# Two batches that take turns on the feed-forward weights: from runs of 8, 16, 8 blocks to runs of 4, 8, 8, 8, 4

## The chip, the cores and the metric

The kernel runs on one core of one Trainium2 chip. The metric is the device time of one execution in microseconds (us), as a median of several runs; less is better. PE is the matrix engine, PEld its weight loads, DVE the vector engine, ACT the scalar engine, SP the engine that issues the DMAs. PSUM is the memory that PE writes to, SBUF the on-chip working memory.

## What is computed

The reference is two stages of attention followed by a feed-forward layer, all in float32 (the inputs are float64 in memory for the two weight matrices, and are turned into float32 on the chip):

```
def sm_attn(qq, kk, vv):
    s = scale * matmul(qq, kk^T);  a = softmax(s);  return a @ vv
p_packed = sm_attn(p, k, v)                 # 32 packed rows per head
out      = sm_attn(q, p_packed, p_packed)
x = out as (B*S, H*D)
h = x @ w_in;  g = h * tanh(softplus(h));  result = g @ w_out
```

There are 8 batches of 8 heads, 576 tokens and a head size of 64; 32 packed rows per head; the feed-forward layer goes from 512 to 2048 (d_ff) and back to 512. h * tanh(softplus(h)) is the Mish function, one ACT instruction here.

## The kernel before

The kernel works batch by batch. For a batch, the attention yields the second-stage softmax weights, transposed, in a high and a low half (`aT_hi`, `aT_lo`: a value and what rounding to the matmul type leaves of it). The second value product is never made alone: `packed_w` (line 428) multiplies the packed values (`ppT`) with a chunk of 512 columns of w_in, again split into halves (`wp_hi` on ACT, `wp_lo` on DVE, lines 446 and 447), and the up-projection multiplies those with `aT`.

**Blocks and steps.** d_ff is cut into 16 blocks of 128. `order` (line 571) lists (batch, block) pairs; a *step* t works on pair t. In a step (line 605) PE makes the up-projection of pair t (`up`, line 477: two halves of 288 tokens, 6 matmuls each, from a PSUM tile `ps_h` through Mish into `g`), and, two steps late (LAG = 2), the down-projection of pair t - 2 (`down`, line 525: four accumulators of 128 tokens, three matmuls each, from the halves `g_hi`, `g_lo` made at lines 498 and 499). Of the 576 tokens, 512 go this way; the last 64 of two batches are gathered over four blocks and multiplied together by `down_rest` (line 545), as soon as both batches have gone through those four blocks.

**Turns.** Batches 2 to 7 go through all 16 blocks in a row. Batches 0 and 1 share the opening, while the weights are still being converted. Line 27 gives their runs:

```
TURNS = [(0, 0, 8), (1, 0, 16), (0, 8, 16)]      # (batch, first block, end)
```

At the end of a run that doesn't end a batch, `evac` (line 509) copies the four accumulators into SBUF tiles `part`; at the end of the batch they are added (line 516) and written out.

**Weight conversion.** w_in and w_out arrive as float64 words. 32 conversions (lines 352 to 419) turn them into float32: 16 of w_in (four chunks of 512 columns by four row blocks) and 16 of w_out (one for each block of d_ff). One conversion is a DMA into a staging tile `w_st` (`fetch`), two ACT instructions (`words`, lines 385 and 386), four DVE instructions (`join`, lines 390 to 397) and `done`: for w_out a cast to the high half on ACT (line 418) and the low half on DVE (line 419), for w_in a DMA that puts every second result into DRAM (line 402), from where batches 2 to 7 and the later turns read it. The list `weights` (line 580) gives the sequence: w_in chunk 0, w_out 0 and 1, w_in chunk 1, w_out 2 to 7, w_in chunk 2, w_out 8, w_in chunk 3, w_out 9 to 15. `conversion` (line 585) hands out half conversions, and `take(conv, n)` places n of them at a point of the program: two in most steps, 42 in all ahead of step 16.

**Order on the engines.** PE's order is the program's order throughout. Until step 16 (START) that holds for DVE, ACT and SP too: every queue is executed in the order written, and an instruction that waits holds up all behind it. From step 16 on the framework orders DVE and ACT by readiness and priority. The attention of batch 1 (`second`) is written out by hand between steps 0 to 4; that of batch 2 is a generator that is stepped from step 20 on (line 613), up to three pieces a step, and must be through by step 30.

## Time and profile before

| | us |
|---|---|
| median of 3 runs (lowest, highest) | 804.06 (804.03, 805.2) |
| the profiled execution | 805.43 |
| its span, first to last instruction | 803.6 |
| PE busy | 765.4 (95%) |
| DVE busy | 441.7 (55%) |
| ACT busy | 322.7 (40%) |

A profile is of one execution. Busy time is the sum of an engine's instruction times; on PE, neighbouring matmuls overlap, so its instructions start closer together than they are long. A row of a timeline gives start, duration, engine, line, operation and tiles; in brackets, how long the engine had been idle and what ended that wait. A row of waits gives who waited for whom, the total, the count and the longest. A row of grouped instructions gives the count, the busy total and the mean in ns. The granted clock is the share of PE's full clock.

### The profile page before, as it was taken

Reading aid. Unit: us, or ns where it says so; the run is one execution under the profiler, and the core shown is the slowest. Engines: PE = TensorE matmul, PEld = TensorE weight load, DVE = VectorE, ACT = ScalarE, POOL = GpSimd, SP = SyncE. Lnnn points to the kernel's source line nnn. Section 1 sums busy time; section 2 is a strip of 40 time slices with the busy share of each in tenths; the row PEclk is TensorE's granted clock in tenths of the full one; section 3 lists DMA queues with packets and bytes.
Section 4 is the critical chain, followed back from the end, with each engine's and each line's share of the span. In section 5 each row is a group of like instructions: output and inputs, shape, how many; then the busy total and the mean of one; then the engine's idle time right before and its main releaser. Section 6 shows DMA issues by size and latency. Waiting matters only on the chain.

```text
span 803.6 us, 13720 instructions
## 1 busy us (share of the span) xinstructions
PE 765.4 (95%) x5584; PEld 610.2 (76%) x5584; DVE 441.7 (55%) x846; ACT 322.7 (40%) x752; POOL 0.7 (0%) x6
## 2 busy tenths in 40 slices
PE   7767689999999999999999999999999999999997
PEld 5445478877887787878788787878788787878886
DVE  5787777696467447353553546444463545542332
ACT  4364557563433424244333433334252343222221
POOL 0000000000000000000000000000000000000000
PEclk7578799999999999999999999999999999999999
DMA  9994105434423441152311541243311501131002
GB/s 263 282 331 156 37 27 171 163 113 118 142 82 117 149 140 56 53 171 79 93 53 61 175 114 60 69 154 112 113 53 53 148 30 54 53 105 53 1 1 66
DMA packets 42814, 85.82 MB, mean 107 GB/s; under 512 B 8448, under 2 KB 26880, under 8 KB 42752
## 3 DMA queue, kind: packets, MB, share of 16 engines
q1 hardware_dynamic: 42752, 84.95, 34.5%
q8 instruction: 44, 0.72, 0.4%
q14 instruction: 18, 0.15, 0.1%
HBM read 71.30 MB, written 13.63 MB: 106 GB/s over the span
## 4 chain that ended last, share of the span: by engine, by line
PE 86%; DVE 8%; ACT 2%; DMA 2%; issue 1%; SPq 0%; DVEq 0%; ACTq 0%
PE ps_h L486 24%; PE acc L503 15%; PE acc L505 14%; PE acc L504 14%; PE ps_kq L120 4%; PE ps_w L435 4%; PE ps_s L129 3%; PE ps_rest L503 2%; PE ps_rest L505 2%; PE ps_rest L504 2%; DMA w_st<-in_moe_w_out_dram 2%; PE ps_pp L260 2%; PE ps_a L251 1%; DVE wo L394 1%; DVE wo L397 1%
## 5 line engine op out<-in xcount | busy, mean ns | idle before, releaser
L503 PE MATMUL acc<-wo,g_hi 128*128 128x512 f32 x512 | 214.6, 419 | 8.0 <-ACT wo L418 5.9
L489 ACT ACTIVATE g<-ps_h 128x288 f32<-128x288 f32 (+1 forms) x256 | 98.2, 384 | 279.7 <-PE ps_h L486 229.1
L504 PE MATMUL acc<-wo,g_hi 128*128 128x512 f32 x512 | 202.9, 396 | 0.2 <-DVE wo L419 0.2
L505 PE MATMUL acc<-wo,g_lo 128*128 128x512 f32 x512 | 203.0, 396 | 0.1
L486 PE MATMUL ps_h<-aT_hi,wp_hi 128*128 128x288 f32 x512 | 158.1, 309 | 2.8 <-ACT g L489 1.8
L498 DVE CAST g_hi<-g 128x512 fp32r<-128x512 f32 x112 | 47.7, 426 | 195.0 <-ACT g L489 195.0
L486 PE MATMUL ps_h<-aT_hi,wp_lo 128*128 128x288 f32 x512 | 152.7, 298 | 1.8 <-DVE wp_lo L447 1.8
L486 PE MATMUL ps_h<-aT_lo,wp_hi 128*128 128x288 f32 x512 | 152.6, 298 | 0.0
L503 PEld LDWEIGHTS acc<-wo,g_hi 128*128 128x128 f32 x512 | 96.9, 189 | 50.3 <-issue 24.0
L505 PEld LDWEIGHTS acc<-wo,g_lo 128*128 128x128 f32 x512 | 97.1, 190 | 22.9 <-DVE g_lo L499 0.5
L486 PEld LDWEIGHTS ps_h<-aT_hi,wp_hi 128*128 128x128 f32 x512 | 97.8, 191 | 19.0 <-issue 5.7
L486 PEld LDWEIGHTS ps_h<-aT_lo,wp_hi 128*128 128x128 f32 x512 | 98.0, 191 | 8.8
L504 PEld LDWEIGHTS acc<-wo,g_hi 128*128 128x128 f32 x512 | 97.4, 190 | 9.2 <-DVE wo L419 1.0
L486 PEld LDWEIGHTS ps_h<-aT_hi,wp_lo 128*128 128x128 f32 x512 | 97.7, 191 | 2.1 <-DVE wp_lo L447 2.1
L499 DVE TENSOR_TENSOR g_lo<-g,g_hi 128x512 fp32r<-128x512 f32 x128 | 88.2, 689 | 12.3 <-ACT g_hi L498 8.1
L447 DVE TENSOR_TENSOR wp_lo<-ps_w,wp_hi 128x512 fp32r<-128x512 f32 x64 | 41.3, 682 | 18.5 <-ACT wp_hi L446 18.4
L446 ACT CAST wp_hi<-ps_w 128x512 fp32r<-128x512 f32 x64 | 34.4, 591 | 28.9 <-PE ps_w L435 28.9
L435 PE MATMUL ps_w<-wi,ppT 64*32 64x512 f32 x512 | 36.2, 615 | 2.0 <-ACT a L223 2.0
L491 ACT ACTIVATE g_rest<-ps_h 128x64 f32<-128x64 f32 x128 | 28.0, 219 | 0.0
L120 PEld LDWEIGHTS ps_kq<-ident,q_t 96*128 96x128 f32 x192 | 22.3, 155 | 7.3 <-issue 3.7
L120 PEld LDWEIGHTS ps_kq<-ident,k_t 96*128 96x128 f32 x192 | 22.3, 156 | 6.6 <-issue 3.3
L112 ACT COPY kT<-ps_kq 128x384 f32<-128x384 f32 x32 | 15.0, 480 | 28.4 <-PE ps_kq L120 28.4
(91 smaller groups left out, 747.7 us busy)
## 6 DMA issues: line engine op xcount, KB each, us to landing
wi<-w_in_f SPq DMA_DIRECT2D x48, 512.0 KB, 4.5
k_t<-in_k_dram SPq DMA_DIRECT2D x32, 288.0 KB, 3.6
q_t<-in_q_dram SPq DMA_DIRECT2D x32, 288.0 KB, 4.2
v_t<-in_v_dram SPq DMA_DIRECT2D x32, 288.0 KB, 3.7
w_st<-in_moe_w_in_dram SPq DMA_DIRECT2D x16, 512.0 KB, 5.8
w_st<-in_moe_w_out_dram SPq DMA_DIRECT2D x16, 512.0 KB, 4.6
out_dram<-o SPq DMA_DIRECT2D x24, 192.0 KB, 2.6
w_in_f<-wi SPq DMA_DIRECT2D x8, 512.0 KB, 4.7
```

Source lines behind the costliest of these rows:

```text
L120: nc.tensor.transpose(out=ps[:, h, :], in_=of_slot(src, g, h)[:, i, :], identity=ident[:R, :R])
L435: nc.tensor.matmul(out=ps[g][h * NP:(h + 1) * NP, :], lhsT=ppTb[row:row + D, g, h * NP:(h + 1) * NP], rhs=wis[c, g][row:row + D, h // 2, : ...
L446: nc.scalar.copy(out=hi, in_=ps[g])
L447: nc.vector.tensor_tensor(out=lo, in0=ps[g], in1=hi.bitcast(F32), op=ALU.subtract)
L486: nc.tensor.matmul(out=ps, lhsT=w[:, fs], rhs=a[:, g, cs], start=(n == 0), stop=(n == 5))
L489: nc.scalar.activation(out=self.act[:, hf * HALF:hf * HALF + m], in_=ps[:, :m], func=AF.Mish)
L491: nc.scalar.activation(out=self.g_rest[self.b % 2, self.f // 4][:, self.f % 4, :], in_=ps[:, m:], func=AF.Mish)
L498: cast(out=hi, in_=self.act)
L499: nc.vector.tensor_tensor(out=lo, in0=self.act, in1=hi.bitcast(F32), op=ALU.subtract)
L503: nc.tensor.matmul(out=acc, lhsT=hi[:, cs], rhs=wh, start=start, stop=False)
L504: nc.tensor.matmul(out=acc, lhsT=hi[:, cs], rhs=wl, start=False, stop=False)
L505: nc.tensor.matmul(out=acc, lhsT=lo[:, cs], rhs=wh, start=False, stop=stop)
```

## The change

The runs become 4, 8, 8, 8, 4 blocks: batch 0 blocks 0 to 3, batch 1 blocks 0 to 7, batch 0 blocks 4 to 11, batch 1 blocks 8 to 15, batch 0 blocks 12 to 15. So batch 1 starts at step 4 instead of step 8, each chunk of w_in is used by both batches in neighbouring runs, and a converted block is needed every second step on average.

The conversions are listed in that sequence: chunk i of w_in, then w_out blocks 4i to 4i + 3. Ahead of step 3, ten half conversions are taken instead of thirteen, and every step from 0 on takes two; 36 are taken ahead of step 16. In the hand-written opening, the second half of batch 1's softmax, transposition and splitting (`weigh`, `back`, `low` of its second head group) moves ahead of step 3.

Batch 0 now stops twice and batch 1 once, so partial sums are also added in place (batch 0 after block 11), and batch 1's live in two tiles of the ring `late` that staging tiles used before; the split w_out blocks 14 and 15 move from that ring to the ring `wstage`. In the hand-written softmax of batches 0 and 1, a maximum and its scaling become one DVE instruction, and so do two additions.

```diff
-TURNS = [(0, 0, 8), (1, 0, 16), (0, 8, 16)]
+TURNS = [(0, 0, 4), (1, 0, 8), (0, 4, 12), (1, 8, 16), (0, 12, 16)]
...
-            nc.vector.tensor_tensor(out=self.top, in0=mx[:, 0:1], in1=mx[:, 1:2], op=ALU.max)
-            nc.vector.tensor_scalar(out=self.top, in0=self.top, scalar1=-scale, scalar2=None, op0=ALU.mult)
+            nc.vector.tensor_scalar(
+                out=self.top, in0=mx[:, 0:1], scalar1=mx[:, 1:2], scalar2=-scale, op0=ALU.max, op1=ALU.mult
+            )
...
-            nc.vector.tensor_tensor(out=rs, in0=sm[:, 0:1], in1=sm[:, 1:2], op=ALU.add)
-            nc.vector.tensor_scalar(out=rs, in0=rs, scalar1=1e-9, scalar2=None, op0=ALU.add)
+            nc.vector.tensor_scalar(
+                out=rs, in0=sm[:, 0:1], scalar1=sm[:, 1:2], scalar2=1e-9, op0=ALU.add, op1=ALU.add
+            )
...
-                wo.append(wts.tile([P, 2, DO], F32R, name=f"wo{self.i}", tag="late", bufs=NF // 2))
+                tag, bufs = ("late", NF // 2) if self.i < NF - 2 else ("wstage", 2)
+                wo.append(wts.tile([P, 2, DO], F32R, name=f"wo{self.i}", tag=tag, bufs=bufs))
...
     def evac(b, acc, c, last):
-        if not last:
-            o = parts[b, c] = wts.tile([P, DO], F32, name=f"part{b}{c}", bufs=1)
+        part = parts.get((b, c))
+        if part is None and not last:
+            if b == 0:
+                part = parts[b, c] = wts.tile([P, DO], F32, name=f"part{c}", bufs=1)
+            else:
+                if c % 2 == 0:
+                    parts[b] = wts.tile([P, 2, DO], F32, name="part_late", tag="late", bufs=NF // 2)
+                part = parts[b, c] = parts[b][:, c % 2]
+            o, part = part, None
+        elif last:
+            o = wts.tile([P, DO], F32, name="o", tag="w2k", bufs=W2K)
         else:
-            o = wts.tile([P, DO], F32, name="o", tag="w2k", bufs=W2K)
-        if (b, c) in parts and last:
-            nc.vector.tensor_tensor(out=o, in0=acc, in1=parts[b, c], op=ALU.add)
+            o = part
+        if part is not None:
+            nc.vector.tensor_tensor(out=o, in0=acc, in1=part, op=ALU.add)
...
-    weights = [Weight(0, m) for m in range(4)] + [WeightOut(0), WeightOut(1)]
-    weights += [Weight(1, m) for m in range(4)] + [WeightOut(i) for i in range(2, 8)]
-    weights += [Weight(2, m) for m in range(4)] + [WeightOut(8)]
-    weights += [Weight(3, m) for m in range(4)] + [WeightOut(i) for i in range(9, NF)]
+    weights = []
+    for i in range(4):
+        weights += [Weight(i, m) for m in range(4)] + [WeightOut(4 * i + m) for m in range(4)]
...
             together(second.turn_weights(1, ps_acc))
-            take(conv, 2)
             together(second.values(1, ps_a))
...
-            take(conv, 2)
+            take(conv, 1)
             step(2, (0, 0, 0), 2, nc.scalar.copy)
             second.weigh(slice(0, 1))
             second.back(0)
             take(conv, 1)
             second.low(0)
-            take(conv, 1)
-            step(3, (0, 0, 0), 2, nc.scalar.copy)
             second.weigh(slice(1, 2))
             second.back(1)
             take(conv, 1)
             second.low(1)
-            take(conv, 1)
-            for t in range(4, START):
-                step(t, (0, 0, 0), {4: 3, 5: 2, 6: 1, 7: 3}.get(t, 2), nc.scalar.copy)
+            for t in range(3, START):
+                step(t, (0, 0, 0), 2, nc.scalar.copy)
```

## The prediction, made before the changed kernel ran

> **What bounds the kernel now.** I read the page first, then the busy time by stretches, then who waited for whom on PE, then the timelines of PE, DVE and ACT where PE has gaps.
>
> ```profile
> span 803.6 us, 13720 instructions
> PE 765.4 (95%) x5584; PEld 610.2 (76%) x5584; DVE 441.7 (55%) x846; ACT 322.7 (40%) x752; POOL 0.7 (0%) x6
> PEclk7578799999999999999999999999999999999999
> ```
> ```profile
> 80.00:90.00 10.00, 3.41 (x9) 2.39 (x10) 8.27 (x15) 5.72 (x12) 0.00 (x0) 0.68 0.23 84
> 110.00:120.00 10.00, 10.00 (x66) 8.20 (x51) 7.59 (x14) 6.18 (x15) 0.00 (x0) 1.00 0.18 52
> ...
> 170.00:180.00 10.00, 8.89 (x62) 6.65 (x60) 9.66 (x20) 7.42 (x18) 0.00 (x0) 1.00 0.33 106
> ...
> 190.00:200.00 10.00, 10.00 (x78) 7.08 (x77) 5.19 (x11) 4.57 (x9) 0.00 (x0) 1.00 0.46 138
> 200.00:220.00 20.00, 20.00 (x180) 16.59 (x178) 9.28 (x19) 9.18 (x21) 0.00 (x0) 1.00 0.50 155
> ```
> The columns are busy us of PE, PEld, DVE, ACT, POOL, then the granted clock. PE is busy 765 of 804 us. The gaps and the low clock lie in the first 110 us; from there PE is full at clock 1.00, but for one place near 176 us. A change to batches 0 and 1 can therefore win only in the opening, and it can lose wherever it crowds DVE while PE is full. PE's own waits, over the whole span and then from 104 us on:
>
> ```profile
> PE acc L503 <- ACT wo L418: 5.9, 1, 5.9
> PE ps_h L486 <- DVE wp_lo L447: 1.8, 1, 1.8
> ...
> PE ps_h L486 <- ACT g L489: 1.1, 1, 1.1
> ```
> The longest wait is for a converted block of w_out. PE's timeline there:
>
> ```profile
> 84.83 0.79 PE L503 MATMUL acc<-wo,g_hi 128*128 128x512 f32 x1 [5.95 <-ACT wo L418]
> 86.58 0.44 PE L486 MATMUL ps_h<-aT_hi,wp_hi 128*128 128x288 f32 x1
> 93.87 0.30 PE L486 MATMUL ps_h<-aT_hi,wp_lo 128*128 128x288 f32 x1
> 103.19 0.50 PE L503 MATMUL acc<-wo,g_hi 128*128 128x512 f32 x1 [2.01 <-ACT g_hi L498]
> 109.66 1.09 PE L435 MATMUL ps_w<-wi,ppT 64*32 64x512 f32 x16
> 113.67 0.30 PE L486 MATMUL ps_h<-aT_hi,wp_hi 128*128 128x288 f32 x1
> 118.06 0.29 PE L486 MATMUL ps_h<-aT_hi,wp_hi 128*128 128x288 f32 x1
> ```
> ```profile
> 113.83 0.80 PE ps_h L486 x6
> ```
> 84.83 opens step 4, 86.58 is that step's first up-projection, 103.19 opens step 6, 109.66 is the packed weight product that closes it. 113.67 and 118.06 are the same instruction of two neighbouring steps: a step at full clock takes 4.39 us. The last fence is from the chain of waits: six up-products take 0.80, 0.133 each, so the 12 down products of a step take 4.39 - 1.60, 0.233 each. Step 6 took 6.47 us from 103.19 to 109.66, 2.1 us more than that: a wait of 2.0 us was enough to lower the clock.
>
> **Part 1, the opening (steps 0 to 6).** The new order needs half the conversions early, so PE no longer waits at step 4 for w_out block 2: its conversion is finished before step 2. But batch 1 now starts at step 4 instead of step 8, so the second half of its attention, both softmax halves and the splits into high and low, must be through DVE and ACT before step 4's first up-projection. I follow the DVE and ACT queues from step 1 on.
>
> ```profile
> 58.18 0.42 DVE L390 TENSOR_SCALAR wi<-wi 128x512 f32<-128x512 f32 x1
> ...
> 59.82 0.69 DVE L397 CUSTOM_DVE_ANT_0 wi<-wi,wround 128x1024 uint16<-128x1024 uint16 x1
> ...
> 64.75 0.48 DVE L277 COPY ppT<-ps_ppT 128x128 f32<-128x128 f32 x2
> 65.84 1.58 DVE L291 STREAM_TRANSPOSE a<-ps_s 128x288 f32<-128x288 f32 x4 [0.61 <-PE ps_s L129]
> ...
> 69.54 0.76 DVE L300 TENSOR_TENSOR a<-a,mx 128x576 f32<-128x576 f32 x1
> ...
> 77.41 0.75 DVE L309 TENSOR_REDUCE sm<-a 128x18 f32<-128x576 f32 x1
> ...
> 79.50 0.78 DVE L319 STREAM_TRANSPOSE at<-a 128x576 f32<-128x576 f32 x1
> 81.01 0.76 DVE L323 TENSOR_TENSOR aT_lo<-at,aT_hi 128x576 fp32r<-128x576 f32 x1 [0.74 <-ACT aT_hi L320]
> ```
> ```profile
> 61.65 0.69 ACT L386 ACTIVATE wround<-w_st 128x512 int32<-128x512 uint32 x1
> ...
> 70.33 0.69 ACT L303 ACTIVATE a<-a 128x576 f32<-128x576 f32 x1 [0.77 <-DVE a L300]
> 70.92 0.65 ACT L385 ACTIVATE wi<-w_st 128x512 f32<-128x512 f32 x1
> 71.48 0.66 ACT L386 ACTIVATE wround<-w_st 128x512 int32<-128x512 uint32 x1
> ```
> ```profile
> L419 DVE TENSOR_TENSOR wo<-wo,wo 128x512 fp32r<-128x512 f32 x16 | 11.0, 689 | 9.0 <-ACT wo L418 9.0
> L418 ACT CAST wo<-wo 128x512 fp32r<-128x512 f32 x16 | 9.9, 616 | 8.0 <-DVE wo L397 7.9
> L489 ACT ACTIVATE g<-ps_h 128x288 f32<-128x288 f32 (+1 forms) x256 | 98.2, 384 | 279.7 <-PE ps_h L486 229.1
> L218 DVE TENSOR_SCALAR top<-top 128x1 f32<-128x1 f32 x4 | 0.6, 154 | 0.1
> ```
> A join is 2.3 us (58.18 to 60.51), the two words on ACT 1.2 us (70.92 to 72.14), a w_out split 0.62 on ACT and then 0.69 on DVE.
>
> Step 1: one join is gone (58.18), but the other one's words now end where 61.65 does, at 62.3, and block 1's split stands behind them: 62.3 + 0.6 + 0.6 + 2.3 + 0.6 for the low half of g puts the ppT copies at 66.4 instead of 64.75, +1.7. The fusions take out eight DVE instructions of 0.15 us (L218 and its like), four in the maxima and four in the sums. The two of batch 1's sums, 0.3, stand closest ahead of this point; all eight would be 1.2. I take 0.6, since DVE waited for others in between and the earlier ones are partly lost there. The transposes so start at 66.9.
> Step 2: transposes and peak take as long as before (65.84 to 70.3, 4.5 us) and end at 71.4; the second exponential, 0.7 us behind, at 72.1. Words, then block 2's cast (ACT, 1.2 + 0.6, to 73.9), its low half, a join (DVE, 0.7 + 2.3, to 76.9), block 3's cast and low half, the low half of g: 78.8.
> Then on DVE: weigh and back, 2.9 us (77.41 to 80.3) to 81.7; a join to 84.0; low, 0.7, to 84.7; the second weigh and back to 87.6. ACT casts until 88.2, then has in its queue two words (1.2), step 3's Mish (2 x 0.38 and a short third, 0.9), two words (1.2), the high half of g and the first half of the packed weights (casts like L418, 0.6 each): 92.7, less some 0.2 because neighbours overlap (70.92 + 0.65 is 71.57, yet the next begins at 71.48): 92.5. All of that stands behind the cast that waits for DVE, and step 4's up-projection needs it: it starts at 92.5 instead of 86.58, **+5.9**, after about 10 us of idle PE. Behind it on PE stand all products of step 4, which nobody needs sooner.
> From there to the packed product that ends step 6 the old kernel took 109.66 - 86.58 = 23.1 us. The new one has no wait for w_out and its conversions go one to a step, the pace at which the old one ran without a gap (110 to 120 us above): 3 x 4.39 less the first down product (0.7) is 12.5, plus a slow clock after the gap. The old stretch from 84.83 to 93.87 held 3.7 us of full-clock work in 7.3 us of running (9.04 less the 1.8 of wp_lo): a loss of 3.6. I take that as one bound and half of it, 1.8, as the other, for the old stretch had the 1.8 us wait in its middle and the new one hasn't; between them, 2.7. That makes 15.2, **-7.9**. Part 1: **-2.0** (bounds -2.9 and -1.1 from the clock alone).
>
> **Part 2, steps 16 to 25: where the conversions went.** By the pace written out (42 half conversions taken by step 16 now, 36 in the new kernel, two a step from there), the last ones are done by step 22 now and by step 25 then, well inside batch 2's attention, which begins at step 20. Before, steps 21 to 26 (190 to 220 us) had 14.5 us of DVE work in 30. Five conversions are added there at the written pace; I count four, since they run ahead of it where ACT and DVE are free: 4 x 2.9 (a join and, for w_out, a low half), and at step 21 four additions of a partial sum, 4 x 0.69 (row L516 below): 28.9 in 30. That is the crowd that 170 to 180 us shows today, 9.66 of 10, with one PE wait of 1.1 us. There are two places where PE's transposes need a PSUM buffer that DVE must read out first (the two score groups of batch 2). Bounds: nothing, if attention goes ahead of the conversions; a join in front of each, 4.6. I take the measured crowd's price at each, 2.2; the old wait at 176 us goes with its bunch of w_out blocks: **+1.1** net.
>
> **Part 3, step 32: batch 2's first up-projection.**
>
> ```profile
> 237.22 1.35 DVE L309 TENSOR_REDUCE sm<-a 128x36 f32<-128x1152 f32 x1 [1.23 <-ACT a L303]
> ...
> 240.25 0.63 DVE L556 TENSOR_TENSOR o_rest<-ps_rest,o_rest 128x512 f32<-128x512 f32 x1
> ...
> 247.30 0.74 DVE L323 TENSOR_TENSOR aT_lo<-at,aT_hi 128x576 fp32r<-128x576 f32 x1
> ```
> ```profile
> 250.47 0.29 PE L486 MATMUL ps_h<-aT_lo,wp_hi 128*128 128x288 f32 x1
> L516 DVE TENSOR_TENSOR o<-acc,part 128x512 f32<-128x512 f32 x4 | 2.7, 686 | 1.0 <-PE acc L505 1.0
> ```
> Batch 2's last low half ends at 248.04 and its reader starts at 250.4: 2.4 us to spare. The change moves the leftover-token product of chunk 2 from step 29 to 25: 12 matmuls of 128x512 at 0.233, which lets PE arrive 2.8 earlier, and its addition (0.63) and a low half, 0.9 of DVE together, leave the chain. Batch 1's output now falls on step 29 with four additions of 0.69, 2.4 us of DVE with their overlap, of which up to 1.2 fits into DVE's wait for the exponential. So 2.4 - 2.8 + 0.9 - (1.2 to 2.4) = a wait of 0.7 to 1.9; I take **+1.4**, nearer the upper end, since the additions come ready one by one while PE runs step 29, mostly before that idle time.
>
> The row at 103.19 has a wait of 2.0 us with a lower clock behind it, the one at 176 us a wait of 1.1 without. The Trainium skill, "TensorE: Matmul & The Clock Gate", Part 1, differs from the first: there the clock halves only after an idle window of some 3.4 us, and by it the second rival below would end at 805.1, without its clock term.
>
> **Costed at nothing:** the other extra evacuations (steps 5 and 13), since PE returns to an accumulator one step (4.39) later and a copy takes 0.7; without that cover 0.7 each. Blocks 14 and 15 in the staging ring and batch 1's partials in the late ring: each takes a buffer whose staged words were joined steps before. On SP the staged loads swap places at the same count; only their own ACT words wait for them, and those now come later. Beyond step 33 nothing changes and PE has no wait.
>
> Sum: -2.0 + 1.1 + 1.4 = **+0.5 us**. The span of the profiled execution would go from 803.6 to 804.1, its own time from 805.43 to 805.9. The median shown, 804.06, lies 1.4 below that execution; on it I forecast **804.6**. About 0.2%, 1.6 us, is what a measurement of this kernel tells from no change.
>
> **Rivals.** *The opening alone counts.* Attention goes ahead of the conversions and the additions fall into idle DVE time: parts 2 and 3 cost nothing, the old 1.1 goes: -3.1, **801.0**. For it: DVE as a whole is at 55%, and one conversion a step goes without a gap at 110 to 120 us. Against: from step 20 PE's order holds the attention's transposes at fixed places. Chance 0.28.
> *The clock drops at step 32.* If the wait there reaches its upper bound, 1.9, it is at the 2.0 us that lowered the clock at 103.19, at a price of 2.1: -2.0 + 1.1 + 1.9 + 2.1 = +3.1, **807.2**. It decides from a wait somewhere between 1.1 (176 us: clock 1.00) and 2.0. For it: the chain has no more slack. Against: 1.4 is below. With a join in front of both places of part 2 it would be 809.6; such cases go with it. Chance 0.35.
> *The change doesn't do what it says.* From step 16 on the order on DVE and ACT is not written by hand; conversions could run ahead of their steps and be over by step 20, as the w_out blocks already do near 170 us. Then part 2 repeats the old wait and the sum is -0.6; this belongs to the forecast's case, which has 0.37.
>
> The range, 800.8 to 808.4, holds all three cases and part of their spread; outside lie the first rival with part 1 at its better bound (-4.0, 800.1) and the second with part 2 near its worst, together about a fifth. Faster by over 0.2%: 0.28; within: 0.37; slower: 0.35.
>
> **What would show it.** Part 1: no PE wait for wo; one PE wait of 8 to 11 us for wp_hi or g before step 4's up-projection; the third packed product 1 to 3 us earlier than 109.66; a wait of about 4 us, not 2.5, for ppT near 66. Part 2: PE waits of about 1 us on ps_kq near 185 and 200 us, behind DVE's subtractions. Part 3: a wait near 250 us of 0.7 to 1.9 on aT, clock 1.00 behind it. Wrong it would be if the gap before step 4 is under 6 us or not there, if PE waits again in steps 5 to 15, or if no PE wait is seen after 180 us.

## The result, and the profile after

The new kernel is slower: 814.18 us median of four runs (812.97 to 815.37) against 804.63 of the old one beside it (804.03 to 806.41), ratio 1.0115 with a 95% interval of 1.0089 to 1.0141. The forecast was 804.6 with a range up to 808.4, so it was wrong. The profiled execution of the new kernel took 813.23 and has a span of 811.5, 7.9 more than the 803.6 before; the executions of one kernel differ by up to 2.4.

The head of the page of the new kernel:

```profile
span 811.5 us, 13710 instructions
PE 764.3 (94%) x5584; PEld 609.3 (75%) x5584; DVE 444.0 (55%) x846; ACT 321.6 (40%) x752; POOL 0.7 (0%) x6
PEclk7577799998999999999999999999999999999999
```

The totals say nothing: PE's work is the same to 1.1 us, DVE's to 2.3. The difference is idle time, and the busy time by stretches shows where it is. First the new kernel, then the row of the old one that answers to the third line:

```profile
80.00:90.00 10.00, 3.46 (x29) 1.73 (x27) 8.85 (x18) 2.85 (x6) 0.00 (x0) 0.81 0.00 0
...
100.00:110.00 10.00, 10.00 (x66) 7.82 (x65) 8.04 (x15) 7.19 (x17) 0.00 (x0) 1.00 0.45 157
...
180.00:190.00 10.00, 6.18 (x48) 4.54 (x48) 9.93 (x24) 6.26 (x15) 0.00 (x0) 1.00 0.56 171
190.00:200.00 10.00, 7.04 (x30) 6.25 (x31) 5.73 (x11) 2.17 (x5) 0.00 (x0) 0.66 0.01 2
```
```profile
180.00:190.00 10.00, 9.97 (x74) 7.89 (x73) 7.54 (x18) 3.38 (x11) 0.00 (x0) 1.00 0.28 74
```

PE is full from 100 us on, ten earlier than before: the opening is shorter. But from 180 to 200 us, where PE was full (9.97, then the 10.00 that the prediction shows), it now works 13.2 of 20 us, part of it at a clock of 0.66, while DVE is full (9.93 of 10). PE's own waits, and then the places in its timeline:

```profile
PE ps_h L489 <- ACT wp_hi L449: 9.0, 1, 9.0
...
PE ps_kq L120 <- issue: 5.2, 1, 5.2
PE ps_s L129 <- DVE ppT L279: 4.0, 1, 4.0
...
PE ps_h L489 <- DVE aT_lo L325: 0.9, 1, 0.9
```
```profile
92.45 0.61 PE L489 MATMUL ps_h<-aT_hi,wp_hi 128*128 128x288 f32 x1 [8.99 <-ACT wp_hi L449]
...
107.13 1.09 PE L438 MATMUL ps_w<-wi,ppT 64*32 64x512 f32 x16
...
180.57 0.52 PE L120 MATMUL ps_kq<-ident,k_t 96*128 96x96 f32 x4 [1.03 <-DVE pT L186]
...
185.39 0.72 PE L129 MATMUL ps_s<-kT,pT 64*32 64x288 f32 x16 [1.04 <-ACT kT L112]
...
192.96 0.87 PE L120 MATMUL ps_kq<-ident,k_t 96*128 96x96 f32 x4 [5.16 <-issue]
...
258.19 0.40 PE L489 MATMUL ps_h<-aT_lo,wp_hi 128*128 128x288 f32 x1 [0.93 <-DVE aT_lo L325]
```

The wait for w_out (5.9) is gone, one of 9.0 for `wp_hi` has come before step 4, and the third packed product, at 109.66 before, is at 107.13. The new costly place is 192.96: the transposes of batch 2's second group of keys, 5.16 us idle. The profile calls the releaser "issue"; the PSUM buffer they need is the one from which DVE subtracts the first group's maximum. DVE at that place, new kernel and then old:

```profile
187.87 0.81 DVE L195 TENSOR_REDUCE mx<-ps_s 128x1 f32<-128x288 f32 x2
188.60 0.41 DVE L395 TENSOR_SCALAR wo<-wo 128x512 int32<-128x512 int32 x1
188.94 0.41 DVE L501 CAST g_hi<-g 128x512 fp32r<-128x512 f32 x1
189.27 0.68 DVE L396 SCALAR_TENSOR_TENSOR wo<-w_st,wo 128x512 int32<-128x512 int32 x1
189.88 0.68 DVE L528 TENSOR_TENSOR part<-acc,part 128x512 f32<-128x512 f32 x1
190.48 0.14 DVE L197 TENSOR_TENSOR top<-mx 128x1 f32<-128x1 f32 x1
190.54 0.68 DVE L396 SCALAR_TENSOR_TENSOR wo<-w_st,wo 128x512 int32<-128x512 int32 x1
191.15 0.68 DVE L502 TENSOR_TENSOR g_lo<-g,g_hi 128x512 fp32r<-128x512 f32 x1
191.75 0.68 DVE L399 CUSTOM_DVE_ANT_0 wo<-wo,wround 128x1024 uint16<-128x1024 uint16 x1
192.35 0.93 DVE L199 TENSOR_SCALAR a<-ps_s,top 128x288 f32<-128x288 f32 x2
```
```profile
187.73 0.82 DVE L195 TENSOR_REDUCE mx<-ps_s 128x1 f32<-128x288 f32 x2 [2.35 <-PE ps_s L129]
188.58 0.16 DVE L197 TENSOR_TENSOR top<-mx 128x1 f32<-128x1 f32 x1
188.78 0.94 DVE L199 TENSOR_SCALAR a<-ps_s,top 128x288 f32<-128x288 f32 x2
```

Before, DVE stood idle until the scores came (2.35) and did maximum, top and subtraction in one go: 1.05 us from the first to the subtraction. Now it takes 4.48. Pieces of two conversions, an addition of a partial sum and the halves of `g` stand ahead of the tiny `top`, and pieces of both conversions and `g_lo` again ahead of the subtraction. Each of the three operations becomes ready only when the one before it has ended, and so stands behind what is ready in the meantime: the queue is paid twice.

The packed products stand at the same places in PE's order in every version here: ahead of step 0 and at the end of steps 3, 6, 10, 14, 18, 22, 26, 30 and 34. From the first to the tenth, in us, by the profiled executions (each stretch holds the same PE work; steps 6 to 18 and 22 to 30 are taken together because a product of leftover tokens changes its place inside them):

| kernel | to step 6 | 6 to 18 | 18 to 22 | 22 to 30 | 30 to 34 | sum |
|---|---|---|---|---|---|---|
| before | 67.46 | 61.81 | 23.52 | 48.78 | 25.03 | 226.60 |
| after | 65.29 | 61.81 | 32.33 | 48.82 | 26.53 | 234.78 |
| difference | -2.2 | 0.0 | +8.8 | 0.0 | +1.5 | +8.2 |

The 8.8 are the three waits above, 7.2, less one of about 1.1 that went, and 2.7 that are left for the lower clock: it was 0.50 from 192.1 to 198.9, and PE worked for 6.0 us of that. And DVE's work was not more. Busy times up to 104 us, to 200 and to 270, before and after:

```profile
0.00:104.00 104.00, 71.47 (x618) 51.94 (x619) 77.28 (x166) 52.42 (x112) 0.70 (x6) 0.72 0.70 207
104.00:200.00 96.00, 94.87 (x582) 76.35 (x583) 72.72 (x139) 56.46 (x130) 0.00 (x0) 0.98 0.39 121
...
sum 270.00, PE 236.32 PEld 184.14 DVE 190.41 ACT 135.34 POOL 0.70; mean PE 78.77 PEld 61.38 DVE 63.47 ACT 45.11 POOL 0.23
```
```profile
0.00:104.00 104.00, 69.58 (x624) 51.04 (x625) 71.43 (x148) 50.09 (x108) 0.70 (x6) 0.72 0.70 193
104.00:200.00 96.00, 88.77 (x526) 72.62 (x525) 76.26 (x146) 55.62 (x130) 0.00 (x0) 0.96 0.41 133
...
sum 270.00, PE 227.36 PEld 177.51 DVE 190.38 ACT 133.11 POOL 0.70; mean PE 75.79 PEld 59.17 DVE 63.46 ACT 44.37 POOL 0.23
```

190.41 and 190.38 in all; 5.9 us of it left the first 104 us, where PE waits anyway, and 3.5 turn up between 104 and 200, where PE is full, 2.3 later.

### The profile page after: what moved, and what is told of

It is laid out like the page before. It is cut to its first block, busy times and chain, and to the rows that moved or that the text cites. A ratio compares the mean times of both kernels' runs of the same rounds, so it can differ in the third digit from the quotient of the medians.

```text
span 811.5 us, 13710 instructions
## 1 busy us (share of the span) xinstructions
PE 764.3 (94%) x5584; PEld 609.3 (75%) x5584; DVE 444.0 (55%) x846; ACT 321.6 (40%) x752; POOL 0.7 (0%) x6
## 4 chain that ended last, share of the span: by engine, by line
PE 82%; DVE 8%; DMA 3%; ACT 3%; issue 1%; SPq 1%; DVEq 0%; ACTq 0%
PE ps_h L489 24%; PE acc L506 15%; PE acc L508 13%; PE acc L507 13%; PE ps_w L438 3%; PE ps_kq L120 3%; PE ps_s L129 3%; DMA w_st<-in_moe_w_in_dram 2%; PE ps_rest L506 2%; PE ps_rest L508 2%; PE ps_rest L507 2%; DMA w_st<-in_moe_w_out_dram 2%; PE ps_pp L262 1%; PE ps_a L253 1%; ACT wround L388 1%
## 5 line engine op out<-in xcount | busy, mean ns | idle before, releaser
L120 PE MATMUL ps_kq<-ident,k_t 96*128 96x96 f32 x192 | 26.3, 275 | 6.3 <-issue 5.2
```

The lines of the kernel that those rows point to most:

```text
L120: nc.tensor.transpose(out=ps[:, h, :], in_=of_slot(src, g, h)[:, i, :], identity=ident[:R, :R])
```

## The experiments

**Theory A**: the loss is DVE's queue in steps 20 to 22, in which what is left of the conversions and four additions stand in front of batch 2's first score group; the clock follows from that wait. **Rival B**: the opening's 9.0 us wait is what costs. **Rival C**: the transfers of the last weight blocks come late because batch 2's loads share the DMA engines. All versions start from the new kernel unless it is said otherwise. Ratios are to the kernel before, run beside each on the same chip. The stretches of all of them stand in one table:

| version | to 6 | 6-18 | 18-22 | 22-30 | 30-34 | sum | median (before) | ratio, 95% interval |
|---|---|---|---|---|---|---|---|---|
| early | 65.92 | 72.38 | 22.13 | 48.76 | 26.55 | 235.74 | 815.37 (806.11) | 1.0110, 1.0095-1.0126 |
| no_add | 65.26 | 61.82 | 30.31 | 48.80 | 26.55 | 232.74 | 812.19 (806.11) | 1.0076, 1.0059-1.0093 |
| load_early | 66.25 | 62.06 | 31.21 | 48.81 | 26.52 | 234.85 | 814.15 (806.11) | 1.0101, 1.0081-1.0120 |
| by_hand | 64.74 | 61.81 | 23.24 | 53.34 | 26.52 | 229.65 | 809.85 (806.11) | 1.0041, 1.0026-1.0056 |
| mid | 65.43 | 68.60 | 22.65 | 48.75 | 26.55 | 231.98 | 811.39 (805.72) | 1.0071, 1.0044-1.0097 |
| hand_first | 66.26 | 61.81 | 24.22 | 55.88 | 26.50 | 234.67 | 814.40 (805.72) | 1.0095, 1.0068-1.0122 |
| open_late | 64.41 | 61.82 | 34.14 | 48.77 | 26.54 | 235.68 | 812.00 (805.72) | 1.0085, 1.0058-1.0112 |
| fused (on before) | 67.17 | 61.80 | 23.58 | 48.73 | 25.05 | 226.33 | 806.59 (805.72) | 1.0009, 0.9996-1.0022 |
| old_pace | 67.67 | 63.19 | 23.61 | 48.77 | 26.50 | 229.74 | 809.65 (806.50) | 1.0032, 1.0011-1.0053 |
| spread | 64.71 | 61.82 | 22.13 | 53.05 | 31.60 | 233.31 | 813.96 (806.50) | 1.0090, 1.0069-1.0111 |
| spread_open | 64.33 | 61.82 | 22.13 | 52.97 | 30.84 | 232.09 | 811.80 (806.50) | 1.0058, 1.0039-1.0076 |
| pool_low | 65.97 | 62.50 | 36.11 | 48.79 | 26.53 | 239.90 | 817.35 (806.89) | 1.0124, 1.0105-1.0142 |
| early_att | 66.26 | 61.82 | 34.79 | 46.79 | 25.01 | 234.67 | 813.54 (806.89) | 1.0077, 1.0059-1.0095 |
| old_early | 66.49 | 62.91 | 30.13 | 47.27 | 25.01 | 231.81 | 811.87 (806.89) | 1.0052, 1.0017-1.0088 |
| old_pool | 67.19 | 64.66 | 32.64 | 47.30 | 25.01 | 236.80 | 815.48 (806.89) | 1.0105, 1.0090-1.0121 |
| act_cast | 65.26 | 61.81 | 30.31 | 48.77 | 26.54 | 232.69 | 812.81 (805.79) | 1.0078, 1.0054-1.0101 |
| old_open | 67.21 | 62.39 | 25.69 | 49.66 | 25.03 | 229.98 | 810.57 (805.79) | 1.0055, 1.0035-1.0075 |
| old_pace_cast | 66.33 | 63.02 | 22.90 | 49.67 | 25.03 | 226.95 | 806.97 (805.79) | 1.0005, 0.9988-1.0022 |

The first column differs by up to 1.5 us between executions of the same opening (64.7 to 66.3 with the new kernel's), so it carries less than the others; where the code is the same, those repeat to 0.3 or better, with two exceptions: steps 18 to 22 of open_late took 1.8 more than the new kernel's (see there), and steps 30 to 34 of spread and spread_open are 0.8 apart (6.8 and 3.4 us at half clock).

### Is it there, and is it DVE's queue?

**early**: conversions earlier.

```diff
-                step(t, (0, 0, 0), 2, nc.scalar.copy)
+                step(t, (0, 0, 0), 3 if 4 <= t < 14 else 2, nc.scalar.copy)
```

> Steps 4 to 13 of the new kernel take three half conversions instead of two, so 46 are taken by step 16 instead of 36. Theory A (DVE's queue in steps 20 to 22 holds the first score group's subtraction up, and the lower clock follows from that wait): the 5.2 us wait on ps_kq near 193 us goes, clock 1.00 there, time 805 to 807, less what the denser steps 4 to 13 may cost (waits up to 2 us). Rival B (the 9.0 us wait of the opening is what costs): 814, unchanged. Rival C (the staged transfers of the last w_out blocks come late because batch 2's loads share the DMA engines): 805 to 807 too, since those transfers come earlier as well; this run does not tell A and C apart.

Steps 18 to 22 took 22.13 instead of 32.33, no wait was left there: the place and the mechanism hold, B's place does not explain it. But the time stayed (ratio 1.0110), against the figure that A had given: steps 6 to 18 lost 10.6. PE's waits of that run between 104 and 170 us:

```profile
PE acc L506 <- ACT g_hi L501: 1.9, 2, 1.2
PE acc L506 <- DVE part_late L532: 1.9, 1, 1.9
PE acc L508 <- DVE g_lo L502: 1.8, 1, 1.8
PE ps_rest L508 <- DVE r_lo L463: 1.2, 1, 1.2
```

The crowd has moved with the conversions. A was right about the place and wrong in taking DVE for free elsewhere.

**no_add**: the four additions at step 21 off DVE. This version leaves the first four blocks of batch 0 out of the sum.

```diff
-        if part is not None:
+        if part is not None and last:
             nc.vector.tensor_tensor(out=o, in0=acc, in1=part, op=ALU.add)
-        elif c % 2 == 0:
+        elif c % 2 == 0 or part is not None:
             nc.scalar.copy(out=o, in_=acc)
```

> The four additions at step 21 (0.68 us each on DVE) become plain copies on ACT, so batch 0's first four blocks of d_ff are left out of the sum; conversions stay where they are. Theory A: DVE has 2.4 us less in front of the first score group's subtraction, the 5.2 us wait falls to 2 to 3, time 809 to 812. B and C: 813 to 815, unchanged.

Steps 18 to 22: 2.0 us less. The wait is 4.4 instead of 5.2, where A had given 2 to 3; all waits there sum to 6.2 instead of 7.2, and half clock lasted 3.4 us instead of 6.8. So the additions are a fourth of the loss at most, and about half of that fourth is clock; B and C, which expected no change, do not explain this.

**load_early**: batch 2's keys, packing vectors and queries loaded at step 10.

```diff
             for t in range(3, START):
+                if t == 10:
+                    batches[2].load_keys()
...
```

> Batch 2's keys, queries and packing vectors are loaded at step 10 instead of step 16, where DMA is nearly idle; only its values are loaded at step 16. DVE's order in steps 20 to 22 stays as it is. Theory A: the wait of 5 us stays within 1.5 us, 812.5 to 814.5. Rival C: the last w_out blocks arrive earlier, conversions are through before 185 us, the wait goes, 806 to 809. B: 814.

`load` at step 16 then brings the values alone. 1.1 us less, but the wait stayed at 5.2 and the three waits at 7.2 in sum; the 1.1 is clock, for more of the half clock (194.0 to 200.9) fell into the wait. In the new kernel itself DVE has no idle time in its rows from 177 to 194 us, so no late transfer held its queue up there. C is not the cause of this wait.

**by_hand**: the written order on DVE and ACT in steps 16 to 23.

```diff
+        with tc.manual_schedule(engines={mybir.EngineType.DVE, mybir.EngineType.Activation}):
+            for t in range(START, 24):
+                if t == 16:
+                    batches[2].load()
+                step(t, (1, 1, 1), 2, nc.vector.tensor_copy)
-        for t in range(START, len(order) + LAG):
+        for t in range(24, len(order) + LAG):
```

> Steps 16 to 23 keep DVE and ACT in the order in which the program is written, as steps 0 to 15 do: two half conversions a step, and a score group's maximum, top and subtraction stand next to each other. The work is the same. Theory A, if it is the order that hurts: the 5.2 us wait is under 1.5 us, time 806 to 808. If it is the amount of DVE work in these steps, whatever its order: the wait moves to another place and the time stays above 811. Rival C: ACT, in order, now waits for late transfers: 811 or more. B: 814.

The same work in another order: steps 18 to 22 took 23.24, 9.1 less. DVE there:

```profile
184.76 0.81 DVE L195 TENSOR_REDUCE mx<-ps_s 128x1 f32<-128x288 f32 x2
185.60 0.16 DVE L197 TENSOR_TENSOR top<-mx 128x1 f32<-128x1 f32 x1
185.80 0.94 DVE L199 TENSOR_SCALAR a<-ps_s,top 128x288 f32<-128x288 f32 x2
```

1.04 from the maximum to the subtraction, as before the change. So the order was what made the queue so dear. But steps 22 to 30 lost 4.5, because ACT in order stands before the exponentials until DVE has done the second group:

```profile
200.71 1.17 ACT L240 ACTIVATE a<-a 128x1152 f32<-128x1152 f32 x1 [4.14 <-DVE a L199]
```

The measured ratio, 1.0041, lies between the two cases that had been written down: 9.1 us go with the order in one place, and half of that comes back at the next.

### Can the conversions go anywhere else?

**mid**: six half conversions more in steps 7 to 14, as many ahead of step 16 as in the old kernel.

```diff
-                step(t, (0, 0, 0), 2, nc.scalar.copy)
+                step(t, (0, 0, 0), 3 if t in (7, 8, 10, 11, 12, 14) else 2, nc.scalar.copy)
```

> Six of the steps 7 to 14 (7, 8, 10, 11, 12, 14) take three half conversions, so 42 are taken by step 16, as in the kernel before, and none of the six lies in steps 4 to 6. Theory A (the queue of conversions and additions on DVE at steps 20 to 22): the stretch from the packed product of step 18 to that of step 22 falls from 32.3 to 24 to 26 us, and steps 7 to 15 lose less than the run with ten extra half conversions did (10.6 us): at most 4. Time 4 to 8 us under the new kernel's, ratio to before 1.001 to 1.006. Rival (a conversion costs the same wherever it is put, since DVE is full everywhere): steps 7 to 15 lose 6 or more and the ratio stays at 1.009 or above.

Steps 18 to 22 took 22.65, 9.7 less; steps 6 to 18 took 6.8 more. Six half conversions in steps that have two already cost 6.8 of the 9.7 that they save, ten in early more than they save. A's limit of 4 us is passed; the rival's ratio isn't reached either.

**hand_first**: as by_hand, but only to step 21.

```diff
-            for t in range(START, 24):
+            for t in range(START, 22):
```

> DVE and ACT keep the written order in steps 16 to 21 only, so that the first score group's maximum, top and subtraction are not parted by conversions, and the exponentials of step 22 are free again. Theory A with order as the cause: steps 18 to 22 take 23 to 25 us, and the 4.5 us that the run with steps 16 to 23 by hand lost in steps 22 to 26 fall to 0 to 2: ratio 1.000 to 1.004. Rival (amount of work): the conversions that are left over crowd the second score group in step 22 and 23, steps 22 to 26 lose 4 or more, ratio 1.004 or above.

Steps 18 to 22 took 24.22, steps 22 to 30 7.1 more than with the new kernel: the rival had it. What the written order keeps away from the first score group meets the second: PE waits 1.74 for `wp_lo` before the second group's scores, and the clock is 0.50 from 203.5 to 210.4.

**old_pace**: the old pace in the new order of turns.

```diff
+            take(conv, 2)
             together(second.values(1, ps_a))
...
-            take(conv, 1)
+            take(conv, 2)
             step(2, (0, 0, 0), 2, nc.scalar.copy)
...
-                step(t, (0, 0, 0), 2, nc.scalar.copy)
+                step(t, (0, 0, 0), 3 if t in (7, 8, 10) else 2, nc.scalar.copy)
```

> The new order of turns with the old pace of conversions: 13 half conversions ahead of step 3 instead of 10 (three more in steps 1 and 2), and three instead of two in steps 7, 8 and 10, so that 42 are taken by step 16 as in the kernel before. Theory A (the new order leaves six half conversions more for steps 16 to 25, and DVE has no room for them there): steps 18 to 22 take 22 to 26 us instead of 32.3. If DVE has room for three of the six in the opening, the first packed product to the third takes at most 1 us more than the new kernel's 65.3, and the ratio is 1.002 to 1.006. Rival (the attention's chain has no room in the opening either): the wait before step 4 grows from 9.0 by 2 to 4 us and the ratio is 1.006 to 1.010.

Two things meet here. Steps 18 to 22 are back at 23.61: the six half conversions left over make the loss there. And the opening takes 67.67, against 67.46 of the old kernel: it has no room, as the rival expected, though the wait before step 4, which was to grow by it, did not (7.5; one of 2.2 on `wp_lo` came behind it). By the mean of all versions here, the stretch to step 6 takes 65.5 with the new kernel's opening (ten versions), 67.0 with three half conversions back (five) and 67.3 with the old order (two): 1.4 of the 1.8 gained hang on those three. Steps 6 to 18 lose 1.4, step 32 still waits. The ratio, 1.0032, lies where theory A had put it for an opening with room.

**spread** and **spread_open**: the written order in steps 16 to 27, conversions just in time.

```diff
+            if self.b == 2:
+                yield
             self.exps(slice(0, 2))
...
+        with tc.manual_schedule(engines={mybir.EngineType.DVE, mybir.EngineType.Activation}):
+            for t in range(START, 28):
...
+                step(t, (1, 1, 1), 1 if 20 <= t < 24 else 2, nc.vector.tensor_copy)
```

> DVE and ACT keep the written order in steps 16 to 27, with one half conversion a step in steps 20 to 23 and two elsewhere, so that each block is ready just ahead of its use; batch 2's first exponentials come one piece of attention later. Same work, other places. Theory A (what costs is DVE's queue in front of the two score groups): no PE wait above 1.5 us from 170 to 240 us, steps 18 to 22 take 21 to 23, steps 22 to 26 26 to 28; ratio 0.998 to 1.003. Rival (amount of work in steps 16 to 27): waits move behind step 23 and the sum of steps 18 to 30 stays 5 us or more above the 75 that full PE would take: ratio above 1.004.

> The run before this one, and the two half conversions of the opening moved to steps 4 and 5 as well. If the two remedies add up: 1 to 2 us less than the run before this one, ratio 0.996 to 1.002. Rival (the moved conversions are paid in steps 4 to 6): the same time as the run before this one within 0.8 us.

Steps 18 to 22 became the shortest of all, 22.13, and the time still did not move: steps 22 to 30 take 53.05 and steps 30 to 34 31.60, since batch 2's attention now ends late. The ratio is the rival's (amount of work). Its other figure is not met: steps 18 to 30 take 75.2, hardly above its 75. But 75 was too much for a full PE; 22.13 here and 48.8 elsewhere make 70.9, so 4.3 are lost. The 5.1 in steps 30 to 34 may come in part from the piece of attention by which this version starts its exponentials later, so the run alone does not show that it is the amount. The opening's two half conversions moved on top gave 0.4 in the first stretch and 1.2 in the sum; the ratio fell from 1.0090 to 1.0058, not to the 0.996 to 1.002 that was given.

**open_late**: the two half conversions between steps 2 and 3 moved to steps 4 and 5.

```diff
             second.back(0)
-            take(conv, 1)
             second.low(0)
...
             second.back(1)
-            take(conv, 1)
             second.low(1)
...
+                step(t, (0, 0, 0), 3 if 4 <= t < 6 else 2, nc.scalar.copy)
```

> The two half conversions that stand inside the second half of batch 1's attention, between steps 2 and 3, move to steps 4 and 5. This tests part 1's reading of the queues. If the 9.0 us wait before step 4 is set by the DVE and ACT queues (a join of 2.3, a low half, two words and a cast): the wait falls to 5 to 7, the third packed product comes 2 to 4 us earlier, ratio 1.007 to 1.009. Rival (the attention's own chain of transposes and exponentials sets it and the conversion lies in its idle time): the wait stays above 8 and the ratio at 1.011.

The wait before step 4 fell from 9.0 to 6.5, inside what reading the queues gave. Only 0.9 of the 2.5 reached the end of step 6, and steps 18 to 22 took 34.14. The ratio, 1.0085, would fit; the stretches of the profiled execution, the slowest of four, do not show that the opening carries it.

Steps 18 to 22 have the new kernel's code here, and from 176 to 198 us DVE has its instructions in the same sequence. Yet they took 1.8 longer:

```profile
189.22 0.43 DVE L392 TENSOR_SCALAR wo<-wo 128x512 f32<-128x512 f32 x1 [1.99 <-ACT wo L387]
...
190.50 0.81 DVE L195 TENSOR_REDUCE mx<-ps_s 128x1 f32<-128x288 f32 x2
```

ACT had stood for 2.36 us until a block's transfer was in, and DVE for 1.99 until ACT was done, while the first group's scores, begun at 186.22 and 0.72 long, lay ready for the maximum. It was written behind that conversion and came at 190.50; PE's wait became 7.0. So the order by readiness is fixed before the program runs, and DVE keeps it even if another instruction could go. And a late transfer, rival C's case, does lengthen the wait in some executions: a difference of less than 2 us in this stretch, from one profile each, says little.

### Taking work off DVE

**pool_low** and **old_pool**: low halves of w_out blocks 8 to 15 on POOL.

```diff
-            nc.vector.tensor_tensor(out=lo, in0=self.dst, in1=hi.bitcast(F32), op=ALU.subtract)
+            by = nc.gpsimd if self.i >= 8 else nc.vector
+            by.tensor_tensor(out=lo, in0=self.dst, in1=hi.bitcast(F32), op=ALU.subtract)
```

> The low halves of w_out blocks 8 to 15 (a subtraction of 0.69 us each, which read and write SBUF alone) go from DVE to the idle POOL; nothing else changes. Theory A (amount of DVE work in front of the score group): the three or four low halves that stood between 180 and 195 us are off DVE, 2 to 3 us, the wait of 5.2 falls to 1 to 3, steps 18 to 22 take 26 to 30 instead of 32.3, ratio 1.004 to 1.009. Rival (POOL and DVE hinder each other, as the Trainium skill has it in Hardware Overview and in GpSimd Engine): DVE's instructions beside a POOL subtraction grow longer by what was saved, ratio 1.010 or above.

It did not get better: 36.11 in steps 18 to 22, and a ratio of 1.0124 against the new kernel's 1.0115, the same within the intervals. POOL and DVE of that run, each with the rows that overlap:

```profile
182.09 1.32 POOL L423 TENSOR_TENSOR wo<-wo,wo 128x512 fp32r<-128x512 f32 x1 [16.39 <-ACT wo L421]
...
194.21 1.26 POOL L423 TENSOR_TENSOR wo<-wo,wo 128x512 fp32r<-128x512 f32 x1 [6.37 <-ACT wo L421]
```
```profile
182.19 1.77 DVE L503 TENSOR_TENSOR g_lo<-g,g_hi 128x512 fp32r<-128x512 f32 x1
...
194.31 1.45 DVE L502 CAST g_hi<-g 128x512 fp32r<-128x512 f32 x1
```

A subtraction of 0.68 on DVE took 1.77 and a cast of 0.42 took 1.45; both began 0.1 after POOL's and ended 0.55 and 0.29 after it. Beside five of the eight subtractions DVE lost 1.0 to 1.1, beside the others 0 to 0.7: 6.3 in all, to save 5.5 (8 x 0.69). The Trainium skill, "SBUF — State Buffer", section "SBUF: two separate sides", has it so: DVE and POOL share one pair of ports, and of a POOL instruction and a DVE instruction that needs the pair, as one with two inputs in SBUF does, whichever begins first keeps it to its end. The trace agrees, by the rows above. (The two titles in the expectation are not titles of the skill; what it says stands on this page.) So this run did not test A.

**act_cast**: the cast of `g_hi` on ACT in steps 16 to 22.

```diff
-            step(t, (1, 1, 1), 2, nc.vector.tensor_copy)
+            step(t, (1, 1, 1), 2, nc.scalar.copy if t < 23 else nc.vector.tensor_copy)
```

> The cast that makes the high half of g goes to ACT in steps 16 to 22 (on ACT it is there in steps 0 to 15 already); 7 times 0.42 us are off DVE, some three of them between 180 and 193 us. Theory A (amount of DVE work): steps 18 to 22 take 28 to 31 instead of 32.3, ratio 1.007 to 1.010. Rival (the order alone, since each of the score's dependent operations queues up again): 32 or more, ratio 1.011.

30.31, 2.0 less, the figure that theory A had given, but not at the place. The wait on `ps_kq` is still 5.4, and from the first group's maximum to its subtraction it takes 4.13 (4.48 in no_add, as in the new kernel). What went is the wait of 1.0 before the first group's transposes, and half clock lasted 3.4 us instead of 6.8. As with the four additions, half of the 2.0 or more is clock. So 2.9 us (7 x 0.42) less work did not shorten the queue inside the chain.

### Step 32, and the remedies together

**early_att** and **old_early**: batch 2's attention from step 19 on; the second with the old pace.

```diff
-            if t == 20:
+            if t == 19:
```

> Batch 2's attention begins at step 19 instead of 20. Part 3's theory (its end decides when step 32 starts): the wait of 0.9 us near 253 us goes, the stretch from the packed product of step 30 to the next one falls from 26.5 to 25.0 to 25.3. In steps 18 to 22 theory A expects the crowd to be no better, since conversions are not through at step 19 either: 30 to 36, ratio 1.008 to 1.015. Rival: the additions of step 21 now come behind the score's subtraction, steps 18 to 22 gain 2 or more, ratio 1.004 to 1.008.

> The old pace of conversions (13 ahead of step 3, 42 ahead of step 16) with batch 2's attention from step 19. If both remedies hold: steps 18 to 22 at 23 to 25, step 30 to the next at 25.0 to 25.3, 1.5 less than the old pace alone, ratio 1.000 to 1.003. Rival (conversions still run at step 19): steps 18 to 22 lose 3 or more, ratio 1.005 or above.

> The run before this one with the low halves of w_out blocks 8 to 15 on POOL as well. Theory A: the 1 to 2 us that steps 7 to 18 lose under the old pace (waits on r_lo and g_lo) shrink, ratio 0.997 to 1.001. Rival (DVE and POOL hinder each other): ratio at or above that of the run before this one.

In all three, steps 30 to 34 take 25.01 instead of 26.53: the wait before step 32 goes when the attention ends earlier. Steps 18 to 22 do not profit (34.79; 30.13 with the old pace, with a wait of 3.9 at the very start of the attention): conversions are not over at step 19. In early_att the wait of 5.2 is down to 1.3, and others of 2.7, 2.2 and 2.8 have come. A part of that is attention work that has moved ahead, since steps 22 to 30 are 1.5 to 2.0 shorter. old_pool, old_early with POOL, lost as pool_low did.

**old_open** and **old_pace_cast**: one piece of attention more in steps 23 to 25, casts on ACT, with three half conversions back in the opening, or the whole old pace.

```diff
-            step(t, (1, 1, 1), 2, nc.vector.tensor_copy)
+            step(t, (1, 1, 2 if 23 <= t < 26 else 1), 2, nc.scalar.copy if t < 23 else nc.vector.tensor_copy)
```

> Three half conversions back in the opening (13 ahead of step 3, then two a step: 39 by step 16), casts on ACT as in the run before, and batch 2's attention takes one piece more in steps 23 to 25. Theory A: steps 18 to 22 take 24 to 28; the opening (first to third packed product) 67 to 68; step 30 to the next 25.0: ratio 1.001 to 1.006. Rival (three conversions left over still crowd the score group): 28 to 32, ratio 1.007 or above.

> The whole old pace (42 by step 16), casts on ACT in steps 16 to 22, and one piece of attention more in steps 23 to 25. If the end of the attention sets step 32: step 30 to the next takes 25.0 instead of 26.5, everything else as in the run with the old pace, ratio 1.000 to 1.003, no better than the kernel before, because the opening's gain is gone and steps 7 to 10 lose 1. Rival: the casts on ACT delay Mish, steps 16 to 22 lose 1 or more, ratio 1.004 or above.

Three half conversions back in the opening give 25.69 in steps 18 to 22, the whole old pace 22.90. PE is full there again:

```profile
180.00:190.00 10.00, 9.92 (x73) 7.73 (x72) 9.07 (x20) 5.28 (x16) 0.00 (x0) 1.00 0.33 95
190.00:200.00 10.00, 9.98 (x80) 7.06 (x80) 5.04 (x10) 5.41 (x12) 0.00 (x0) 1.00 0.21 59
```

With these remedies together (old pace, casts on ACT, attention a piece faster) the new order of turns takes 806.97 against 805.79, ratio 1.0005 (0.9988 to 1.0022): the same as the old kernel. No version here beats it.

**fused**: the old kernel with the two fused operations alone.

> The kernel before with the two fused DVE operations alone, eight instructions of 0.15 us fewer. The prediction took 0.6 us for them: ratio 0.9985 to 1.0000. Rival (some of them lie in waits for PE or ACT): nothing, 0.9998 to 1.0002.

Ratio 1.0009 (0.9996 to 1.0022), sum of the stretches 0.3 less: nothing that can be measured.

## Why the prediction was wrong

**Part 1, the opening, was right.** Forecast -2.0, measured -2.2 in the stretches. Step 4's up-projection was put at 92.5 and began at 92.45, after 9.0 us of idle PE where "about 10" was written; the third packed product at 107.7 and came at 107.13; the wait for `ppT` of 4 us was 4.0. open_late moved that wait by 2.5 when two half conversions were taken out of the queue. That the times agree to 0.05 us is luck in part, since the first packed product moves by up to 4.5 us between executions and came at 42.20 and 41.84 in these two. Counted from it, the up-projection was forecast 50.3 later and came 50.6 later, and the third product 65.5 and 65.3. The 0.6 us for the fusions was not confirmed.

**What was costed at nothing** cost nothing: steps 6 to 18 take 61.81 in both kernels.

**Part 3 was right.** Forecast +1.4, measured +1.5, with a wait of 0.9 on `aT_lo` (the rest is in the products next to it, which stand further apart); early_att showed that the end of the attention sets it.

**Part 2 is the step that failed**: +1.1 net was forecast, +8.8 measured. The step that failed is the price of two places "where PE's transposes need a PSUM buffer that DVE must read out first": 1.1 us each, from the crowd at 176 us in the old kernel, with one join in front of each, 4.6, as the upper bound. One of the two places took 5.2, with two waits of 1.0 ahead of it and a lower clock behind; the other took nothing. Three things were missing.

First, the old crowd stood in front of single operations. A score group is a chain, maximum, top, subtraction, and in an order made by readiness every link queues up anew: 4.48 us from the first to the last where there is a backlog, 1.05 without, and 1.04 in by_hand with the same work. An upper bound of one join for a chain of three was too low.

Second, the work was spread over steps 21 to 26, "28.9 of 30" us of DVE. The conversions ran ahead of their written steps, as the last rival said, but that was no relief: the last ones all stood in steps 20 to 22, with the four additions, ahead of the first score group (by no_add the additions make 2.0 of the 8.8, half of it clock). DVE was busy for 9.93 of 10 us from 180 on and for 5.73 of the next 10: worse than forecast at the first group, better at the second.

Third, the prediction put the danger of a lower clock only at step 32. It came at 192 us, with a wait of 5.2, and cost 2.7. The prediction had taken the wait of 2.0 before 103.19 as enough by itself; the last section shows what the clock went by.

Behind this stands an omission in the whole sum. The opening's gain was counted as a gain, and its source, conversions taken later, as a separate small cost. They are the same 5.9 us of DVE work. old_pace shows it from one side: with three half conversions back, most of the opening's gain is gone. early and mid show it from the other: in steps 4 to 14 ten and six half conversions cost 10.6 and 6.8 us of PE time, for 10.2 and 9.7 saved.

What stays open: how much of the 8.8 is order and how much amount. The order alone takes 9.1 out of steps 18 to 22, but never without giving 4 us or more back behind them; no run had both the written order and less work there. An arrangement of these conversions that gains was not found, which does not show that there is none.

## What to carry to other kernels

Before counting a gain from work that is put off, add up the busy time of the engine that does it, by stretches, and look where it will land: what leaves a stretch in which the main engine waits anyway and arrives where it is full is a loss, even at 55% over the whole span. Price a crowd on a side engine by the chain that must pass through it, the backlog once for each dependent operation, not by a single wait measured elsewhere. When a wait vanishes under a new order, sum the next stretches too; here it came back there, in whole or in part, each time that only the order had changed.

## What the runs showed of the hardware that I had not expected

**The clock does not go by the longest wait, but by PE's busy share in fixed windows.** In early_att a wait of 2.7 us left the clock at 1.00; in spread two of 1.0 and 1.5, three us apart, halved it. Busy PE and granted clock, two us a row, spread and then early_att:

```profile
250.00:252.00 2.00, 1.42 (x7) 0.81 (x5) 1.67 (x3) 0.29 (x1) 0.00 (x0) 1.00 0.39 154
252.00:254.00 2.00, 0.93 (x3) 0.48 (x3) 1.59 (x4) 1.15 (x4) 0.00 (x0) 1.00 0.00 0
254.00:256.00 2.00, 0.61 (x1) 0.29 (x1) 1.83 (x3) 0.67 (x1) 0.00 (x0) 0.51 0.00 0
256.00:258.00 2.00, 1.92 (x6) 1.72 (x7) 0.58 (x4) 0.41 (x1) 0.00 (x0) 0.50 0.00 0
```
```profile
174.00:176.00 2.00, 0.00 (x0) 0.00 (x0) 1.27 (x3) 2.00 (x5) 0.00 (x0) 1.00 0.93 287
176.00:178.00 2.00, 1.67 (x9) 1.38 (x10) 2.00 (x7) 0.35 (x2) 0.00 (x0) 1.00 1.00 365
```

A later wait of early_att, 2.8 before 200.33, was followed by half clock from 201.9 on.

In each run the clock changes on a grid of 3.41 us only. In the new kernel it fell at 65.8, 76.1, 86.3 and 192.1 and rose at 69.2, 79.5, 96.5 and 198.9: all distances are multiples of 3.41, and half clock lasts 3.4, 6.8 or 10.2 us there. The Trainium skill, "TensorE: Matmul & The Clock Gate", Part 1, speaks of a window of activity of about 3.4 us that runs freely. The traces agree with that.

What counts is how much of such a window PE is busy. I took the windows at full clock between 60 and 285 us in all twenty profiles, with the busy time as the profile gives it. The 61 with PE busy for less than 0.48 of the window were all followed by half clock, the 1053 with more than 0.52 never; of the eight between, two were. The wait of 2.7 fell so that its window still had 0.485, that of 2.8 into one of 0.45, and the two short ones of spread into one of 0.51. The prediction's threshold, between a wait of 1.1 and one of 2.0, is therefore not what decides: ahead of 104.1, where the clock fell in the old kernel, PE was busy for 0.39 of the window, in pieces. A drop costs whole windows, so the same wait can be followed by 3.4 or by 6.8 us at half clock.

**A subtraction on POOL can hold DVE up to its end** (pool_low above): 1.0 to 1.1 us lost for 0.69 saved, beside five of eight.

**The opening's start differs by executions.** With the same instructions ahead of it, the first packed product came between 40.37 us (mid) and 44.88 us (load_early).
